# Moving a routing head, two gathers and three turns of gathered rows within the last batches of a retention and expert kernel

## The chip, the core and the metric

The kernel runs on one core of a Trainium2 chip. The metric is the device time of one execution in microseconds (us). Engines are TensorE (PE in the profile; PEld is its weight loads), VectorE (DVE), ScalarE (ACT), GpSimd (POOL) and SyncE (SP), which issues most transfers.

## What is computed

The reference is causal retention followed by a layer of experts with one expert per token:

```python
scores = (q @ k.transpose(0, 1, 3, 2)) / sqrt(64)            # (8, 8, 576, 64) each
ret = scores * Dmat        # Dmat[h, i, j] = gamma[h] ** (i - j) for i >= j, else 0
x = (ret @ v).transpose(0, 2, 1, 3).reshape(4608, 512)
logits = norm(x) @ norm(expert_emb).T / tau                  # 8 experts
expert = argmax(logits, axis=1)
gate = softmax(logits)[token, expert]
out = gate * (relu(x @ w1[expert]) @ w2[expert])             # 512 -> 1024 -> 512
```

All data is float32; the large products are made from high and low parts, each of which TensorE takes at its faster float32 form.

## The kernel before, in words

The work has two stages. The first loops over the eight batches of the retention (b = 0 to 7) and routes tokens to experts on the way; the second loops over the eight experts. Inside a scheduled region the order of each engine's instructions is the order in which the program emits them, so the order is written out by hand, and SP's and POOL's queues keep it too.

For every batch from 1 on the program calls `scores(b)`, `tokens(b - 1)` and `products(b)`. The 576 positions of a batch are four chunks of 128 and a tail of 64; heads go in four pairs.

- `scores(b)`: per pair, `emit_A` (L703) makes the scores within each chunk on TensorE (L709) and evicts them on DVE times the decay (L718); `scale_q` (L697) scales the queries of the pair on POOL (L699), in place, after the scores have read them. At the end `scale_k` (L676) scales the keys of the next batch on POOL, four instructions (L680) that wait for the load of these keys. In batch 7, three gathers (`gather`, L357, POOL's L360) come directly behind the first scaling of queries: each fetches 128 token rows of expert 0 from `xd` in HBM, by the indices `gid`, into the buffers raw2, raw3 and raw6.
- `tokens(b)`: `route_logits` (L892) makes the logits of the batch, evicted by ACT (L903); `route_rank(b - 1)` (L246) ranks the tokens of the batch before within their experts: TensorE multiplies with the one-hots (L256 to L260) into a PSUM bank, DVE adds up the counts (L263, L267), reads the bank (L270), and makes slot numbers (L273 to L284); `route_onehot` (L287) makes two more one-hots on DVE (L292, L300, L307); `route_tile` (L868) turns a tile of 128 tokens on TensorE (L875), copies it on ACT (L876) and stores it to `xd` from SP (L879); `route_turn` (L907) turns the logits and adds them up on DVE (L917). In tokens(6), which stands in front of products(7), `xprep` (L387) follows for each of the three gathered blocks: four transposes on TensorE (L392) into one PSUM bank, a high part by ACT (L384) and a low part by DVE (L385); behind each `w0_load` (L511) issues a load of 512 KB of expert 0's first weights from SP (L513) into the first part of the same raw buffer, which overlaps the gathered rows.
- `products(b)`: `emit_U` (L726) makes the state sums: TensorE (L736) into two PSUM banks, one copy on ACT (L746) and three running sums on DVE (L748). In batch 6 `route_bump`, `route_table(4)` and `slots_to_tokens(0, 3)` (L339 to L350) come next, which make the indices of the three gathers. `emit_O` (L784, L792) makes the outputs within chunks, in two groups of two pairs. `route_squares` (L884) squares the batch's tiles on ACT (L887). In batch 7 `w0_high` (L515) rounds the first two blocks of weights on ACT (L518) and the low parts follow behind `emit_At` on DVE and POOL (L519). `emit_At` (L824) makes the scores of the tail, times the decay on DVE (L833). Then comes the **routing head**, `route_head(b - 1)` (L179): six small DVE instructions (L191, L192, L194, L196, L198, L199) that find each token's expert. `emit_S` (L800, L808) adds the state's part to the outputs, which ACT evicts (L818, L821, L822; DVE the last group of batch 7), and `emit_Ot` (L838, L848) the tail's outputs, evicted by DVE (L859). In batch 7 the head stands behind `emit_Ot`.

PSUM has eight banks. From batch 1 on `Banks.tile` hands them out in one ring, in the order of the calls; whoever writes a bank waits until its former content has been read. After batch 7 the first product of an expert, `mm1_in` (L450, L457), starts; it needs the high and the low parts of the three turned blocks and of the first weights. Between such products stand the logits, ranks, turns and heads of the last batches (L1030 to L1048).

Of the kernel before, what the change touches and what calls it, by code (L numbers as in the profile page):

```python
# [9 lines left out]
F32 = mybir.dt.float32  # L10
# [8 lines left out]
P = 128  # L19
B, H, S, D = 8, 8, 576, 64  # L20
NP = H // 2
NCH = 4
# [71 lines left out]
def retention_moe(ctx: ExitStack, tc: tile.TileContext, qk, kv, w1, w2, head, cst, out):  # L94
# [22 lines left out]
    psa, psm, every = Banks(banks[:4]), Banks(banks[4:]), Banks(banks)  # L117
# [237 lines left out]
    BEG = group_tiles(B - 3)[0] * P  # L355

    def gather(e, i, rows=N):  # L357
        a = e * CT + i
        t = xg[e, i] = raws[(2, 3, 6)[i]] if (e, rows) == (0, BEG) else raws[(i + 1) % 7]
        nc.gpsimd.indirect_dma_start(  # L360
            out=t[:, XO : XO + DM],
            out_offset=None,
            in_=xd[:rows, :],
            in_offset=bass.IndirectOffsetOnAxis(ap=gid[:, a : a + 1], axis=0),
        )
# [18 lines left out]
        nc.scalar.copy(hi, u)  # L384
        nc.vector.tensor_tensor(out=x[:, 1, :, j * P : (j + 1) * P], in0=u, in1=hi.bitcast(F32), op=ALU.subtract)  # L385

    def xprep(e, i):  # L387

        t = xg.pop((e, i))
        ps = psm.tile([P, 512], F32, name="m")  # L390
        for p in range(NP):
            nc.tensor.transpose(ps[:, p * P : (p + 1) * P], t[:, XO + p * P : XO + (p + 1) * P], ident)  # L392
        xsplit(i, ps.rearrange("p (r n) -> p r n", r=NP))
        done(ps)
# [107 lines left out]
    with ExitStack() as att:  # L502
# [8 lines left out]
        def w0_load(c):  # L511
            w0[c] = raws[(2, 3, 6, 5)[c]][:, :1024]
            nc.sync.dma_start(out=w0[c], in_=w1[0, c])  # L513
# [162 lines left out]
        def scale_k(b):  # L676
            g = cc("gneg").rearrange("p (c h) -> p c h", c=NCH)
            k = kview(b).rearrange("p c (h d) -> p c h d", h=H)
            for c in range(NCH):
                nc.gpsimd.tensor_tensor(  # L680
                    out=k[:, c], in0=k[:, c], in1=g[:, c].unsqueeze(2).broadcast_to([P, H, D]), op=ALU.mult
                )
# [42 lines left out]

        def emit_U(b):  # L726
            k, v, T = kview(b), vview(b), Tst
            for c2 in range(NCH // 2):
                ps = psm.tile([P, 512], F32, name="m")
                u = ps.rearrange("p (c r d) -> p c r d", c=2, r=NP)  # L730
                for ci in range(2):
                    c = 2 * c2 + ci
                    for p in range(NP):
                        for h in range(2):
                            hd = 2 * p + h
                            nc.tensor.matmul(  # L736
                                u[h * D : (h + 1) * D, ci, p, :],
                                k[:, c, hd * D : (hd + 1) * D],
                                v[:, c, hd, :],
                                start=True,  # L740
                                stop=True,
                            )
                for ci in range(2):
                    c = 2 * c2 + ci
                    if c == 0:
                        nc.scalar.copy(T[:, 0], u[:, 0])  # L746
                    else:
                        nc.vector.tensor_tensor(out=T[:, c], in0=u[:, ci], in1=T[:, c - 1], op=ALU.add)  # L748

        def emit_U0(g):  # L750
            k, v, T = kview(0), vview(0), Tst
# [212 lines left out]
        def scores(b):  # L964
            for p in range(NP):
                emit_A(b, p)
                scale_q(b, p)
                if (b, p) == (B - 1, 0):
                    for i in range(3):
                        gather(0, i, BEG)  # L970
            if b + 1 < B:
                scale_k(b + 1)

        def tokens(b):
            route_logits(b)
            if b >= 1:
                route_rank(b - 1)
            if 2 <= b < B - 2:
                route_table(b - 2)
            if b >= 1:  # L980
                route_onehot(b - 1)
            for g in range(group_tiles(b)[1]):
                route_tile(b, g)
            route_turn(b)
            if b == B - 2:
                for i in range(3):
                    xprep(0, i)
                    w0_load(i)

        def products(b):  # L990
            end = b == B - 1
            emit_U(b)
            if b == B - 2:
                route_bump()
                route_table(b - 2)
                slots_to_tokens(0, 3)
            emit_O(b, 0)
            emit_O(b, 1)
            route_squares()
            if end:  # L1000
                low = [w0_high(0), w0_high(1, nc.gpsimd)]
                w0_load(3)
            emit_At(b)
            if end:
                for split in low:
                    split()
            else:
                route_head(b - 1)
            emit_S(b, 0)
            emit_S(b, 1)  # L1010
            emit_Ot(b)
            if end:
                split = w0_high(2)
                route_head(b - 1)
                split()
# [13 lines left out]
        b = B - 1  # L1029
# [20 lines left out]
    with ExitStack() as moe:  # L1050
# [98 lines left out]
        highs, lows, held = [], [], []  # L1149
# [179 lines left out]
        b = B - 1  # L1329
# [240 lines left out]
```

## Time and profile before

| what | value |
|---|---|
| median of 3 runs | 571.63 us (570.49 to 573.10) |
| the profiled execution | 571.3 us |
| its span, first to last instruction | 569.3 us |
| busy share of the span, TensorE | 98% |
| weight loads of TensorE | 89% |
| DVE | 74% |
| ACT | 68% |
| POOL | 42% |

The profile is of one execution. Busy time counts the instructions of an engine, overlapping weight loads apart. An arrow `<-` at the end of a row, in brackets, names what ended the idle time in front of it; "issue" is idle time in which the engine waited for nothing that the profile shows. The retention fills the span's first 138 us; the experts follow.

### The profile page before, as it was taken

What the parts mean: (1) busy time and instruction counts of PE and PEld (TensorE: products, weight loads), DVE (VectorE), ACT (ScalarE), POOL (GpSimd) and SP (SyncE); (2) the same over time, 40 slices, a digit from 0 to 9 for tenths busy, and PEclk for the clock granted to TensorE, in tenths of its full rate; (3) what the DMA queues carried; (4) which work ended last, traced back from release to release, by engine and by line L of the source; (5) the groups of instructions that cost most, each with busy time, mean ns of one, the idle gap of its engine ahead of it and who ended that gap; (6) DMA issues with size and microseconds to landing.
All of it is one profiled execution on the core that took longest, in us unless ns stands there. A gap on an engine that the chain in (4) does not pass through costs nothing.

```text
span 569.3 us, 13083 instructions
## 1 busy us (share of the span) xinstructions
PE 558.0 (98%) x5090; PEld 506.5 (89%) x5090; DVE 420.0 (74%) x938; ACT 384.5 (68%) x700; POOL 237.8 (42%) x233
## 2 busy tenths in 40 slices
PE   8999999998999999999999999999999999999995
PEld 8899989887998899889989988998898899889985
DVE  5767767998866878877877878688687878887810
ACT  1345555555749887887787788778878887867511
POOL 6674443574346740552075037306521750342022
PEclk9999999999999999999999999999999999999999
DMA  9999999956567583557457445735655585423211
GB/s 324 413 374 377 364 380 337 384 184 209 181 203 172 183 191 120 168 167 161 130 156 194 129 136 172 172 112 168 181 133 144 168 162 171 116 93 90 70 41 46
DMA packets 72128, 109.22 MB, mean 192 GB/s; under 512 B 42328, under 2 KB 43772, under 8 KB 70272
## 3 DMA queue, kind: packets, MB, share of 16 engines
q1 hardware_dynamic: 62960, 86.24, 48.8%
q0 software_dynamic: 7696, 19.95, 10.8%
q10 hardware_dynamic: 1408, 2.17, 1.1%
q8 instruction: 41, 0.67, 0.5%
q14 instruction: 23, 0.19, 0.1%
HBM read 80.27 MB, written 19.94 MB: 176 GB/s over the span
## 4 chain that ended last, share of the span: by engine, by line
PE 88%; issue 8%; DVE 2%; POOL 1%; DMA 1%; POOLq 0%; ACT 0%; SPq 0%; DVEq 0%
PE m L1248 22%; PE a L1195 15%; PE a L1248 11%; PE m L1195 11%; PE a L457 3%; PE a L709 3%; PE a L792 3%; PE m L792 2%; PE m L709 2%; PE m L457 2%; PE m L875 2%; PE a L736 1%; PE m L736 1%; PE m L808 1%; PE a L875 1%
## 5 line engine op out<-in xcount | busy, mean ns | idle before, releaser
L1248 PE MATMUL m<-w2s,hs 128*128 128x512 f32 x600 | 138.8, 389 | 0.0
L1248 PEld LDWEIGHTS m<-w2s,hs 128*128 128x128 f32 x600 | 112.3, 188 | 22.9
L1261 POOL DMA_INDIRECT out<-y,sid x41 | 47.5, 1159 | 191.9 <-DVE wsum L1117 125.7
L1248 PE MATMUL a<-w2s,hs 128*128 128x512 f32 (+1 forms) x384 | 83.6, 376 | 0.0
L1248 PEld LDWEIGHTS a<-w2s,hs 128*128 128x128 f32 x384 | 68.9, 188 | 13.1
L1195 PE MATMUL a<-xsb,w0s 128*128 128x320 f32 x342 | 58.0, 309 | 0.0
L373 POOL DMA_INDIRECT gt<-gd,gid x40 | 45.1, 1128 | 19.2 <-issue 10.5
L1195 PEld LDWEIGHTS a<-xsb,w0s 128*128 128x128 f32 x342 | 52.1, 188 | 0.0
L360 POOL DMA_INDIRECT raw<-xd,gid x40 | 42.9, 1072 | 20.8 <-DVE sid L350 9.2
L1166 ACT ACTIVATE hs<-y 128x320 fp32r<-128x320 f32 x84 | 39.3, 474 | 17.8 <-DVE y L1207 16.7
L1159 DVE SCALAR_TENSOR_TENSOR hs<-y,hs 128x320 fp32r<-128x320 f32 x84 | 46.7, 569 | 2.0
L408 ACT COPY raw<-raw 128x1024 uint16<-128x1024 uint16 x35 | 47.5, 1356 | 0.0
L443 ACT CAST xsb<-raw 128x128 fp32r<-128x128 f32 x70 | 32.1, 459 | 21.7 <-DVE raw L426 20.9
L680 POOL TENSOR_TENSOR kt<-kt,cs 128x512 f32<-128x512 f32 x28 | 28.3, 1043 | 42.3 <-DMA kt<-kv 42.3
L1094 DVE TENSOR_TENSOR w2s<-raw,w2s 128x1024 fp32r<-128x1024 f32 x32 | 39.1, 1223 | 7.0 <-ACT w2s L1091 7.0
L1207 DVE TENSOR_TENSOR y<-a,y 128x320 f32<-128x320 f32 x47 | 22.8, 488 | 19.9 <-ACT y L1211 13.6
L1091 ACT CAST w2s<-raw 128x1024 fp32r<-128x1024 f32 x32 | 33.4, 1045 | 3.2 <-DMA raw<-w 3.2
L401 ACT COPY raw<-raw 128x1024 uint16<-128x1024 uint16 x35 | 35.4, 1046 | 0.0
L699 POOL TENSOR_TENSOR qkt<-qkt,gsb 128x384 f32<-128x384 f32 x32 | 31.3, 1005 | 7.6 <-PE a L709 4.0
L419 DVE TENSOR_TENSOR raw<-raw 128x256 f32<-128x256 f32 x35 | 14.8, 424 | 26.1 <-ACT raw L408 26.1
L1195 PE MATMUL m<-xsb,w0s 128*128 128x320 f32 x198 | 34.1, 309 | 0.0
L1211 ACT COPY y<-a 128x320 f32<-128x320 f32 x48 | 20.5, 426 | 16.8 <-PE a L1195 12.7
(254 smaller groups left out, 1200.4 us busy)
## 6 DMA issues: line engine op xcount, KB each, us to landing
raw<-w SPq DMA_DIRECT2D x64, 512.0 KB, 3.9
qkt<-qk SPq DMA_DIRECT2D x28, 576.0 KB, 7.3
xd<-y SPq DMA_DIRECT2D x36, 256.0 KB, 9.5
vt<-kv SPq DMA_DIRECT2D x7, 1152.0 KB, 12.9
kt<-kv SPq DMA_DIRECT2D x7, 1024.0 KB, 10.5
qkt<-qk ACTq DMA_DIRECT2D x4, 288.0 KB, 5.4
qkt<-qk SPq DMA_DIRECT2D x4, 288.0 KB, 5.6
out<-y,sid POOLq DMA_INDIRECT x41, 3.1
```

Of the source, the lines that this page charges most:

```text
L360: nc.gpsimd.indirect_dma_start(out=t[:, XO : XO + DM], out_offset=None, in_=xd[:rows, :], in_offset=bass.IndirectOffsetOnAxis(ap=gid[:, a ...
L373: nc.gpsimd.indirect_dma_start(out=g[:, i : i + 1], out_offset=None, in_=gd[:, :], in_offset=bass.IndirectOffsetOnAxis(ap=gid[:, a : a + 1 ...
L401: nc.scalar.copy(far.rearrange("p (h n) -> p h n", h=2), near.rearrange("p (n h) -> p h n", h=2))
L408: nc.scalar.copy(far.bitcast(U16).rearrange("p (n h) -> p h n", h=2), near.rearrange("p (h n) -> p h n", h=2))
L443: nc.scalar.copy(hi, u)
L1091: nc.scalar.copy(hi, u)
L1094: nc.vector.tensor_tensor(out=lo, in0=u, in1=hi.bitcast(F32), op=ALU.subtract)
L1159: nc.vector.scalar_tensor_tensor(out=lo, in0=part(src), scalar=0.0, in1=hi.bitcast(F32), op0=ALU.max, op1=ALU.subtract)
L1166: nc.scalar.activation(hi, part(src), AF.Relu)
L1195: nc.tensor.matmul(ps[:, :HC], w[:, ws, ka, d * P : (d + 1) * P], xop(kx, xsp)[:, d, :], start=(n in (1, 2, 5) and d == 0 and k == 0), sto ...
L1248: nc.tensor.matmul(ps[:, :step], hs[:, hsp, f, i * P : (i + 1) * P], w[:, ws, f, n : n + step], start=(j == 0 and k == 0), stop=(j == NF - ...
L1261: put = nc.gpsimd.indirect_dma_start(out=out.rearrange("t (k n) -> (t k) n", k=k), out_offset=bass.IndirectOffsetOnAxis(ap=rows, axis=0), ...
```

## The change

It takes the two PSUM tiles of the state sums before their first use and hands them back from `emit_U`. The routing head of every batch but the last is called directly behind the state sums instead of behind the scores of the tail; in batch 6 that is in front of `route_bump`, `route_table` and `slots_to_tokens`. In batch 7, gathers 1 and 2 are issued behind the last scaling of queries, gather 0 stays where it was. The turn of gathered block 0, with its weight load, goes behind the state sums, those of blocks 1 and 2 between the two groups of outputs, into the two PSUM banks of the state sums. The head of batch 7's products stays behind `emit_Ot`.

```diff
-    def xprep(e, i):
+    def xprep(e, i, ps=None):
 
         t = xg.pop((e, i))
-        ps = psm.tile([P, 512], F32, name="m")
+        if ps is None:
+            ps = psm.tile([P, 512], F32, name="m")
...
         def emit_U(b):
             k, v, T = kview(b), vview(b), Tst
-            for c2 in range(NCH // 2):
-                ps = psm.tile([P, 512], F32, name="m")
+            held = [psm.tile([P, 512], F32, name="m") for _ in range(NCH // 2)]
+            for c2, ps in enumerate(held):
...
+            return held
...
                 scale_q(b, p)
                 if (b, p) == (B - 1, 0):
-                    for i in range(3):
-                        gather(0, i, BEG)
+                    gather(0, 0, BEG)
             if b + 1 < B:
                 scale_k(b + 1)
+            else:
+                for i in (1, 2):
+                    gather(0, i, BEG)
...
             route_turn(b)
-            if b == B - 2:
-                for i in range(3):
-                    xprep(0, i)
-                    w0_load(i)
+
+        def first_row(i, ps=None):
+            xprep(0, i, ps)
+            w0_load(i)
 
         def products(b):
             end = b == B - 1
-            emit_U(b)
+            held = emit_U(b)
+            if not end:
+                route_head(b - 1)
             if b == B - 2:
                 route_bump()
                 route_table(b - 2)
                 slots_to_tokens(0, 3)
+            if end:
+                first_row(0)
             emit_O(b, 0)
+            if end:
+                for i, ps in enumerate(held, 1):
+                    first_row(i, ps)
             emit_O(b, 1)
             route_squares()
...
             if end:
                 for split in low:
                     split()
-            else:
-                route_head(b - 1)
             emit_S(b, 0)
```

## Rows read from the trace of the kernel before

**Rows 1.** Busy time by stretch: us, busy (instructions) of PE, PEld, DVE, ACT, POOL, clock, DMA, GB/s
```profile
138.50:172.90 34.40, 34.40 (x271) 32.87 (x269) 25.40 (x76) 20.47 (x41) 16.04 (x11) 1.00 0.55 175
```

**Rows 2.** Waits of PE from 20 to 172 us: us in total, times, longest
```profile
PE m L392 <- DVE t L273: 1.3, 1, 1.3
```

**Rows 3.** Timeline of POOL in batch 7: start, us, engine, line, operation, out<-in, count
```profile
121.73 1.18 POOL L360 DMA_INDIRECT raw<-xd,gid  x1 [0.18 <-DVE raw L718]
...
125.46 2.92 POOL L699 TENSOR_TENSOR qkt<-qkt,gsb 128x384 f32<-128x384 f32 x3
```

**Rows 4.** Timeline of DVE in batch 7 and behind it
```profile
125.53 2.89 DVE L267 TENSOR_TENSOR run<-run,s 128x8 bf16<-128x8 bf16 x1
...
129.53 0.83 DVE L292 TENSOR_TENSOR bt<-ai,iota 128x640 bf16<-128x640 int32 x1
...
136.01 1.22 DVE L519 TENSOR_TENSOR w0s<-raw,w0s 128x1024 fp32r<-128x1024 f32 x1
...
142.39 0.24 DVE L331 TENSOR_TENSOR tab<-m,tab 128x80 f32<-128x80 f32 x1 [0.80 <-PE m L258]
...
145.34 0.20 DVE L198 TENSOR_TENSOR oh<-wm,wme 128x40 bf16<-128x40 f32 x1
```

**Rows 5.** Timeline of PE in batch 7 and behind it
```profile
128.87 0.63 PE L392 MATMUL m<-ident,raw 128*128 128x128 f32 x4 [1.32 <-DVE t L273]
...
133.09 1.92 PE L792 MATMUL m<-raw,vt 128*64 128x128 f32 x32
...
138.50 2.36 PE L457 MATMUL a<-xsa,w0s 128*128 128x384 f32 x12
...
145.87 0.19 PE L256 MATMUL m<-oh,stri 128*128 128x40 bf16 x1
```

**Rows 6.** L194 by source line (ns: least/median/most), then DVE's and POOL's timelines beside batch 1
```profile
L194 DVE SCALAR_TENSOR_TENSOR w<-L_all,wme x8: 192/584/969, 35.8 to 144.9; 128x32 f32<-128x32 f32 x4, 128x40 f32<-128x40 f32 x4
...
37.67 1.05 DVE L199 TENSOR_SCALAR tok_all<-wm 128x4 f32<-128x4 f32 x1
...
34.66 4.05 POOL L680 TENSOR_TENSOR kt<-kt,cs 128x512 f32<-128x512 f32 x4 [3.12 <-DMA kt<-kv]
```

**Rows 7.** L360 by source line with landings, then timelines of a later gather and of DVE
```profile
L360 POOL DMA_INDIRECT raw<-xd,gid x40: 944/954/1885, 121.7 to 459.2; - x40
...
DMA to landing us min/median/max: 3.3/3.7/5.6
...
157.62 1.89 POOL L360 DMA_INDIRECT raw<-xd,gid  x1 [0.19 <-issue]
...
157.39 1.22 DVE L1094 TENSOR_TENSOR w2s<-raw,w2s 128x1024 fp32r<-128x1024 f32 x1
```

**Rows 8.** ACT's squares (first, last) and rounding, SP's loads; landings of weight loads
```profile
130.90 0.64 ACT L887 ACTIVATE junk<-y 128x512 bf16<-128x512 f32 x1
...
133.70 0.19 ACT L887 ACTIVATION_READ_ACCUMULATOR junk<-y 128x1 f32 x1
134.40 1.05 ACT L518 CAST w0s<-raw 128x1024 fp32r<-128x1024 f32 x1 [0.51 <-DMA raw<-w]
...
128.03 7.35 SPq L513 DMA_DIRECT2D raw<-w  x4
...
raw<-w SPq DMA_DIRECT2D x64, 512.0 KB, 3.9
```

**Rows 9.** Timeline of PEld in the tokens of batch 1, one of two such rows
```profile
43.36 0.42 PEld L875 LDWEIGHTS m<-ident,xT 128*128 128x128 f32 x4 [0.18 <-DVE raw L718]
```

**Rows 10.** Timelines of POOL, DVE and PEld in batch 6's products
```profile
113.50 4.04 POOL L680 TENSOR_TENSOR kt<-kt,cs 128x512 f32<-128x512 f32 x4 [5.97 <-DMA kt<-kv]
...
112.62 0.88 DVE L748 TENSOR_TENSOR Tst<-m,Tst 128x256 f32<-128x256 f32 x2
...
117.67 0.41 DVE L833 TENSOR_TENSOR pt<-a,cd 128x256 f32<-128x256 f32 x1
...
118.53 0.26 PEld L848 LDWEIGHTS m<-pt,vt 64*64 64x64 f32 x8
```

## The prediction

> **What bounds the kernel now.** I first read the busy time by stretch. From 138.5 us on TensorE is busy for all 34.40 us of the stretch [rows 1]: behind batch 7 it has no hole, so the end can only move by what TensorE gains or loses before that point. Second, the waits of TensorE between 20 and 172 us: one wait for another engine stands there, 1.3 us in the turning of gathered rows (L392) for DVE's L273 [rows 2]; its other holes are "issue", where the profile shows nothing waited for, and the change removes nothing of those. Third, the queues of POOL and DVE around that wait. POOL issues three gathers and only then does the last three scalings of queries, 125.46 to 128.38 [rows 3]. The count of the one-hots on DVE (L267), which reads two SBUF operands, starts at 125.53 and takes 2.89 us [rows 4]: it ends with the third scaling. Behind it in DVE's queue stands the read that gives the ranking's bank back, and the third turn wanted that bank. So TensorE paid 1.32 us, at 128.87 [rows 5], for the order on POOL. The same thing on a smaller scale: L194 of the routing head (two SBUF operands) takes 0.19 us alone and up to 0.97 us [rows 6], beside a scaling of keys; L199, one operand, took 1.05 us in the same place in batch 1's head [rows 6].
>
> **The change, part by part.**
>
> *The PSUM tiles of the state sums taken up front, and two of them used again for turned rows.* The ring is walked in the same order; two fewer banks are taken. No instruction is added: nothing. The cover is that DVE has read both banks before TensorE returns to them; worked out below, it has.
>
> *Gathers 1 and 2 behind the scalings.* On POOL gather 0 ends at 122.91 (121.73 + 1.18); three scalings take 2.92 us [rows 3], so they end at 125.83 where they ended at 128.38. L267 then waits for the last of them alone: it ends at about 125.88 instead of 128.42, 2.54 us earlier, and everything behind it on DVE with it. The 1.32 us on TensorE are gone. Gather 1 follows at about 126.0, gather 2 (0.95 us and a gap of 0.2 on [rows 7]) at 127.2; a gather lands 3.7 us after its start in the median, 5.6 at most [rows 7]: 130.9 for the second.
>
> *The turns moved between sums and outputs.* Same work, other place. From the start of the second pair of outputs to the first expert product TensorE takes 138.50 - 133.09 = 5.41 us [rows 5]. Without the 1.32 us the product could start at 137.18, the second pair of outputs at 131.77, and a turn costs 0.55 us, so TensorE wants gather 2 at 131.22, after its landing at 130.9. What is late next? The gather could be. DVE's L292, also with two SBUF operands, now runs from 126.99 to 127.82 (129.53 less 2.54, 0.83 us [rows 4]), and gather 2 starts inside it. A gather that started 0.23 us into the two-operand L1094 took 1.89 us instead of the median 0.95 [rows 7]: it waited until that instruction ended. Here 0.6 us would be left: landing 131.5, and TensorE waits w = 0.2. I take that, as the row is of the same kind; the ends are 0 and, with a landing of 5.6 us, 1.6.
>
> The Trainium skill (SBUF — State Buffer, "Who interferes with whom") infers that a tensor_tensor of DVE holds only the shared read interface while a gather's descriptors need the write interface, so that it shouldn't delay one. By that w would be 0 and the sum 0.2 us lower; the 1.89 us speak against it.
>
> *The weight loads behind the turns.* The squares (2.99 us, 130.90 to 133.89) and the rounding of the first weights on ACT, 1.05 us [rows 8], now stand behind the third turn's copy, taken as 0.6 us: 131.77 + 0.6 + 2.99 + 1.05 = 136.4, and DVE's low part (1.22 [rows 4]) ends at 137.6 + w, 0.4 us later than before (137.23). The first expert product needs it in its third matmul, due at 137.18 + 0.4: just met. So 1.3 us of slack are used up. Load 0 is issued at about 128.9 (the first turn's end) instead of 128.03; before, it landed about 6.3 us on, when ACT's wait ended at 134.40 [rows 8], now then at 135.2, before ACT is free at 135.35. Load 1 is issued at 131.2: at 3.9 us (the median of 64 such loads [rows 8]) it is hidden; at 6.3 it comes at 137.5, 1.1 us after ACT wants it, and ACT's copies of the first outputs wait behind it, which the batch's logits need: some 0.5 us more. I take 0, since no stores stand in front of it on SP any more; 0.5 belongs to the range.
>
> Then DVE sets the pace. From the end of its first low part to the end of L198 at 145.54 are 8.31 us, of which at least 0.80 waiting for TensorE [rows 4]: 7.5 us of work, so L198 ends at 145.1 + w. The ranking that needs it started on TensorE at 145.87 [rows 5] and could now start at 144.55. So 0.55 us of the 1.32 are given back here. Batch 7: 1.32 - 0.55 - 0.2 = about **-0.6 us** (from -1.3, nothing given back, to +1.3, with the late gather and the late load).
>
> *The routing head behind the state sums.* In batch 1 the head stood beside scaling and held the evictions of batch 2's scores back; TensorE's turns of tiles waited for them, 0.18 us at 43.36 and as long once more behind it [rows 9]. That goes: -0.4. In the other batches TensorE waits for no eviction behind the head: nothing. In batch 6 it can lose. The sums end there at 113.50 (112.62 + 0.88), and in the same moment POOL starts four scalings of keys, 113.50 to 117.54 [rows 10]. Now, four waiting instructions of the slots' arithmetic absorb these, and the decay product (L833) starts at 117.67, ends at 118.08, and TensorE's tail outputs want it at 118.53 [rows 10]. After the change the head's L192, L194, L198 and L199 meet the four scalings, one each, and the head ends at 117.57; behind it come the slots' nine small instructions, unheld (0.17 each, 1.5 us) and the product, 0.41: 119.4, so TensorE is 0.9 us late. But it comes 0.4 earlier from batch 2: if the scalings, which wait for a load, do not move, L192 slips in ahead of them, one scaling is left for a later instruction, and the end is only about 0.3 late against before. Bounds for the end of batch 6: -0.4 (no meeting) to +0.9. I take **+0.3**, the case that moves with TensorE and not with the load.
>
> **Sum.** +0.3 - 0.6 = -0.3 us. The profiled execution took 571.3 us, span 569.3 and 2.0 around it: 571.0. The three runs shown have a median of 571.63, from 570.49 to 573.10, so this execution lies 0.3 under the median. That the two stretches differ by less than the runs scatter is the forecast: no measurable change. About 0.5%, 2.9 us, is what a measurement of this kernel can tell from no change.
>
> **Rivals.**
>
> *All of it arrives* (0.22). Neither the low parts nor the head are ever late: -0.4 - 1.3 = -1.7, 569.6. For it: the weights' loads may land in 3.9 us and the scalings of keys in batch 6 may start later. Against it: DVE's chain behind the first low part.
>
> *The head is caught by the scalings of keys* (0.18), the other side. Place: DVE behind batch 6's sums. The price: if L192 loses every boundary between scalings, as L267 did for 2.89 us, it waits to 117.57, the rest of the head takes 1.0, the slots 1.5, the product 0.4: 120.5 against 118.53, +2.0; with the gain of batch 7, 572.7; without, 573.3. It decides as soon as scalings start before L192 (0.25 us behind the sums). For it: L267. Against it: in batches 1 to 5 each held instruction of the head ended with one scaling [rows 6].
>
> The Trainium skill (SBUF — State Buffer, "SBUF: two separate sides") calls the port between DVE and GpSimd an exclusive lock, held for one whole instruction by whoever starts first. By that L267 would have waited about 1.0 us and not 2.89, and this rival would cost 0.9 instead of 2.0; the trace shows both lengths.
>
> *The gather or the second load is late* (0.10). Landing at 5.6 us gives w = 1.6; the load adds 0.5: 571.3 + 0.3 - 0.6 + 1.9 = 572.9.
>
> The forecast, both effects half undone, keeps 0.50; its own range is 570.2 to 572.2.
>
> **How the numbers follow.** The range goes from the first rival less run scatter to the second plus little: 569.3 to 573.3. Over 2.9 us either way needs more than any single mechanism gives, or a shift of the holes called issue: faster 0.08, same 0.86, slower 0.06.
>
> **What would show it.** Right: L267 of batch 7 at 0.2 to 0.5 us; no wait of L392 for DVE; ACT's rounding of the first weights ending about 136.4 and TensorE's first expert product slowed or started near 137.2; DVE without idle time from there to L198; L192, L194, L198 in batch 6 near 1 us each and L833 later than 118. Wrong: if the first expert product starts 1.5 us earlier and its ranking too (all arrives), if L392 waits for a gather, or if TensorE idles over 1 us in front of batch 6's tail outputs. And all of it is wrong if the stretch behind 138.5 changes its own length.

## The result and the profile after

| | median | runs | ratio to the kernel before, 95% interval |
|---|---|---|---|
| before | 570.52 us (568.91 to 573.48) | 22 | |
| after | 574.47 us (570.62 to 579.12) | 22 | 1.0053 [1.0037, 1.0069] |

The change costs about 3 us by the ratio, 0.53% (4 us between the two medians). The forecast was 571.0 with a range up to 573.3; it was wrong. The profiled execution of the changed kernel took 579.12 us (span 577.1), the longest of its 22, so it shows the loss large; the same kernel profiled a second time ("again" below) took 573.98. One run of head_back (692.5 us) and one of the kernel before (815.9 us), both at a much lower granted clock, stand in none of the ratios.

Waits of TensorE over the whole span, changed kernel: line waited for, us in total, times, longest. [Rows 2] held the wait for DVE's L273 instead.

```profile
PE m L393 <- DMA raw<-xd,gid: 2.4, 1, 2.4
```

The wait for DVE is gone, as meant, and a wait for a gather of 2.4 us stands in its place. The timeline of TensorE in batch 7 of the changed kernel has it (against [rows 5]; L393, L794, L458 are L392, L792, L457 of before):

```profile
131.00 1.39 PE L737 MATMUL m<-vt,kt 128*64 128x64 f32 x40
132.62 0.32 PE L737 MATMUL m<-vt,kt 128*64 128x64 f32 x3 [0.24 <-issue]
133.34 0.85 PE L737 MATMUL m<-vt,kt 128*64 128x64 f32 x21 [0.40 <-issue]
134.12 0.66 PE L393 MATMUL m<-ident,raw 128*128 128x128 f32 x4
134.71 1.97 PE L794 MATMUL a<-raw,vt 128*64 128x128 f32 x32
136.60 0.66 PE L393 MATMUL m<-ident,raw 128*128 128x128 f32 x4
139.63 1.09 PE L393 MATMUL m<-ident,raw 128*128 128x128 f32 x4 [2.37 <-DMA raw<-xd,gid]
140.65 3.09 PE L794 MATMUL a<-raw,vt 128*64 128x128 f32 x32
...
148.43 1.06 PE L902 MATMUL a<-xT,E 128*32 128x512 f32 x8
```

The third turn waits for gather 2 from 137.26 to 139.63. Then it takes 1.09 us where the second took 0.66, and the second pair of outputs 3.09 us where the first took 1.97, for the same 32 matmuls. The busy time by stretch says why; its eighth number is the granted clock:

```profile
137.00:140.60 3.60, 1.23 (x7) 0.74 (x5) 0.69 (x1) 0.58 (x1) 0.00 (x0) 0.86 0.66 239
140.60:143.60 3.00, 3.00 (x33) 2.85 (x32) 0.69 (x1) 2.75 (x8) 0.00 (x0) 0.60 0.52 176
143.60:149.00 5.40, 5.40 (x120) 4.59 (x120) 4.12 (x11) 4.55 (x9) 2.81 (x2) 1.00 0.30 104
```

Behind the idle time TensorE ran for a while at the lower of its two levels, 1.2 instead of 2.4 GHz (mean 0.60 in the second row; 1.00 from 134.10 to 137.00), and was back at full clock behind it. Where gathers 1 and 2 stand is seen on POOL's timeline of the changed kernel (against [rows 3]):

```profile
130.59 1.00 POOL L360 DMA_INDIRECT raw<-xd,gid  x1 [0.17 <-issue]
131.89 1.36 POOL L360 DMA_INDIRECT raw<-xd,gid  x1 [0.31 <-issue]
```

and what they meet on SP's and on DVE's timelines (two fences; the second answers to [rows 4]):

```profile
129.97 1.81 SPq L881 DMA_DIRECT2D xd<-y  x4
```

```profile
130.05 0.40 DVE L267 TENSOR_TENSOR run<-run,s 128x8 bf16<-128x8 bf16 x1
...
131.60 0.83 DVE L292 TENSOR_TENSOR bt<-ai,iota 128x640 bf16<-128x640 int32 x1
```

L267 takes 0.40 us instead of 2.89. But between 129.97 and 131.78 SP issues four stores of 256 KB to `xd`, the tiles of `tokens(6)`, gather 1 is issued among them and gather 2 right behind. The transfers of the changed kernel from 131.7 to 133.0, by queue (q1 carries SP's transfers, q0 the gathers; packets, MB, share of the 16 engines' time):

```profile
q1 hardware_dynamic: 249, 0.45, 94.4%
q0 software_dynamic: 1, 0.00, 5.6%
```

While gather 1 has been issued, 249 packets of stores go and one of the gather's, which starts at 132.9. Not all of that is the stores' doing: with the stores out of the way (stores_behind, below) the first packet of this gather comes 0.6 us into the answering stretch, so the stores put it off by some 0.6 us. Behind it both queues go side by side; the changed kernel from 134.25 to 134.75:

```profile
q0 software_dynamic: 33, 0.12, 58.4%
q1 hardware_dynamic: 36, 0.07, 37.8%
```

**Where the time went.** One length sorts all kernels below: from the start of batch 7's scores to the start of the logits behind the first expert product (L710 and L902 in the changed kernel). It was 21.57 us before and is 24.67 here. What lies behind it is the same: 428.5 us before, 428.7 after. So [rows 1]'s reading holds, and the loss is batch 7's, +3.1 us. (What lies in front is 119.2 and 123.8 us. Of these 4.5 us, 2.3 are idle time in more and longer stops called "issue", one of them 1.64 us at L810, and 2.2 are longer busy time; the other profiles have 118.3 to 120.8 in front.) A second profile with batch 7 as before, that of head_alone below, has a stretch of 20.14, so the 3.1 may be too small by up to 1.4. The parts of the 3.1: the wait for the gather 2.37; the lower clock 1.12 and 0.43, by the rows above; two stops called "issue" inside the state sums, 0.64; gone are the old wait of 1.32 and a stop of 0.73, also "issue", that the kernel before had in the tail of batch 7. That makes 2.5; most of the other 0.6 us is found below.

### The profile page after: what moved, and what is told of

Read it like the earlier page. It is cut to its first block, busy times and chain, and to the rows that moved or that the text cites. A ratio compares the mean times of both kernels' runs of the same rounds, so it can differ in the third digit from the quotient of the medians.

```text
span 577.1 us, 13084 instructions
## 1 busy us (share of the span) xinstructions
PE 562.5 (97%) x5090; PEld 510.0 (88%) x5090; DVE 414.4 (72%) x938; ACT 384.1 (67%) x700; POOL 234.7 (41%) x233
## 4 chain that ended last, share of the span: by engine, by line
PE 85%; issue 8%; DMA 2%; POOL 2%; DVE 2%; ACT 1%; POOLq 0%; SPq 0%; DVEq 0%; ACTq 0%
PE m L1257 17%; PE a L1257 16%; PE m L1204 14%; PE a L1204 13%; PE a L710 4%; PE a L458 2%; PE m L710 2%; PE a L794 2%; PE m L794 2%; PE m L458 2%; DMA raw<-xd,gid 1%; PE m L877 1%; PE a L877 1%; PE a L737 1%; PE m L737 1%
## 5 line engine op out<-in xcount | busy, mean ns | idle before, releaser
L1257 PE MATMUL m<-w2s,hs 128*128 128x512 f32 (+1 forms) x528 | 119.3, 384 | 0.0
L1257 PEld LDWEIGHTS m<-w2s,hs 128*128 128x128 f32 x528 | 97.4, 188 | 19.4
L1257 PE MATMUL a<-w2s,hs 128*128 128x512 f32 (+1 forms) x456 | 103.1, 384 | 0.0
L1257 PEld LDWEIGHTS a<-w2s,hs 128*128 128x128 f32 x456 | 83.9, 188 | 16.7
L360 POOL DMA_INDIRECT raw<-xd,gid x40 | 43.4, 1086 | 19.8 <-issue 7.9
L373 POOL DMA_INDIRECT gt<-gd,gid x40 | 42.5, 1062 | 18.5 <-issue 10.5
L1204 PE MATMUL a<-xsb,w0s 128*128 128x320 f32 x294 | 49.3, 309 | 0.0
L1204 PEld LDWEIGHTS a<-xsb,w0s 128*128 128x128 f32 x294 | 44.7, 188 | 0.0
L1204 PE MATMUL m<-xsb,w0s 128*128 128x320 f32 x246 | 41.6, 309 | 0.0
L1204 PEld LDWEIGHTS m<-xsb,w0s 128*128 128x128 f32 x246 | 37.5, 188 | 0.0
L1204 PE MATMUL m<-xsb,wsa 128*128 128x320 f32 x198 | 33.8, 309 | 0.0
```

Source lines behind the costliest of these rows:

```text
L360: nc.gpsimd.indirect_dma_start(out=t[:, XO : XO + DM], out_offset=None, in_=xd[:rows, :], in_offset=bass.IndirectOffsetOnAxis(ap=gid[:, a ...
L373: nc.gpsimd.indirect_dma_start(out=g[:, i : i + 1], out_offset=None, in_=gd[:, :], in_offset=bass.IndirectOffsetOnAxis(ap=gid[:, a : a + 1 ...
L1204: nc.tensor.matmul(ps[:, :HC], w[:, ws, ka, d * P : (d + 1) * P], xop(kx, xsp)[:, d, :], start=(n in (1, 2, 5) and d == 0 and k == 0), sto ...
L1257: nc.tensor.matmul(ps[:, :step], hs[:, hsp, f, i * P : (i + 1) * P], w[:, ws, f, n : n + step], start=(j == 0 and k == 0), stop=(j == NF - ...
```

## The experiments

Each group of kernels had its own runs of the kernel before, whose medians were 571.4 (head_back, head_alone, gathers_early and again), 572.0 (loads_behind to gather2_later) and 572.0 (the last four). "Stretch" is the length just defined, "rest" what lies behind it, both in the one profiled execution; a 0.001 of the ratio is 0.57 us.

| kernel | median, us | ratio [95% interval] | stretch, us | rest, us |
|---|---|---|---|---|
| before | 570.5 | 1 | 21.57 | 428.5 |
| after | 574.47 | 1.0053 [1.0037, 1.0069] | 24.67 | 428.7 |
| again (after once more) | 573.53 | 1.0038 [1.0017, 1.0059] | 23.79 | 428.9 |
| head_back | 574.71 | 1.0056 [1.0028, 1.0084] | 21.73 | 429.0 |
| head_alone | 570.89 | 0.9992 [0.9977, 1.0007] | 20.14 | 428.6 |
| gathers_early | 572.93 | 1.0028 [1.0008, 1.0047] | 21.97 | 428.9 |
| loads_behind | 574.12 | 1.0044 [1.0017, 1.0071] | 23.61 | 428.9 |
| squares_first | 571.60 | 0.9994 [0.9973, 1.0015] | 20.75 | 428.5 |
| gathers_first | 570.03 | 0.9958 [0.9933, 0.9982] | 18.73 | 428.6 |
| gather2_later | 575.42 | 1.0059 [1.0035, 1.0084] | 24.57 | 428.4 |
| stores_behind | 574.27 | 1.0029 [0.9998, 1.0060] | 21.14 | 430.5 |
| front_all | 571.49 | 0.9987 [0.9964, 1.0010] | 20.59 | 428.8 |
| front_squares | 571.05 | 0.9976 [0.9950, 1.0001] | 19.35 | 429.5 |
| front_head | 569.54 | 0.9953 [0.9925, 0.9981] | 18.99 | 428.7 |

### again: the change once more

> The changed kernel once more, for a second profile. In the first one TensorE waited 2.4 us for the second of the two late gathers, the granted clock fell behind that wait, and batch 6's tail came 0.6 us later against before. Theory A (late gather): the wait for the gather is there again, 1.5 to 3 us, and time over before is 2 to 4 us. Theory B (the routing head is caught by the scalings of keys in batch 6): the wait in batch 7 is small or absent this time, and batch 6 loses 1 us or more.

0.4% slower again, and its wait of L393 for the gather was 1.93 us. TensorE kept its full clock behind that one (1.00 in every stretch), and the second pair of outputs took its 1.97 us. Without the clock's loss another wait is to be seen; TensorE's timeline of this second execution:

```profile
134.79 0.63 PE L393 MATMUL m<-ident,raw 128*128 128x128 f32 x4 [1.93 <-DMA raw<-xd,gid]
...
139.92 0.62 PE L458 MATMUL m<-xsa,w0s 128*128 128x384 f32 x2 [0.22 <-ACT w0s L519]
141.18 2.00 PE L458 MATMUL m<-xsa,w0s 128*128 128x384 f32 x10 [0.64 <-DVE w0s L520]
```

The first expert product waits 0.86 us for the rounded weights. In the slower execution above, these came in time because TensorE was later still.

Something other than stores stands in front of the gather's end here. Two rows of this execution's transfers from 132.25 to 134.2 (q8, "instruction", carries fetches of instructions, 16 KB each):

```profile
q0 software_dynamic: 4, 0.01, 3.3%
q8 instruction: 1, 0.02, 2.8%
```

The fetch starts at 132.26; no packet of a gather starts between 132.3 and 133.1, and the last four follow it, behind 133.1. In the first execution the last one likewise follows a fetch, after a gap from 137.4 to 138.25. So some 0.9 us of the gather's lateness there, and up to 1.9 here, stand behind a fetch and not behind stores (that fetch and packets share a DMA engine is read from their times alone). In loads_behind, below, no fetch stands near the gather's end.

### head_back and head_alone: which half loses?

head_back is the changed kernel with the head at its old place; head_alone is the kernel before with the head moved.

```diff
# head_back, against after          # head_alone, against before
-            if not end:              +            if not end:
-                route_head(b - 1)    +                route_head(b - 1)
...
+            else:                    -            else:
+                route_head(b - 1)    -                route_head(b - 1)
```

> The changes of batch 7 alone: the routing head stands behind the scores of the tail again, in all batches. Theory A: all of the loss stays, +2 to +4 us over the kernel before, with TensorE waiting 1.5 to 3 us for a gather. Theory B: the loss goes, within 0.5 us of before, or a gain up to 1 us.

> The kernel before with nothing but the routing head moved directly behind the state sums; gathers and turns as before. Theory A: within 1 us of the kernel before (-0.4 from batch 2, up to +0.9 in batch 6). Theory B: +2 us or more.

The whole loss stays with the first and none with the second: it is batch 7's part. The head does meet the scalings of keys in batch 6; DVE's timeline of head_alone there:

```profile
114.14 0.74 DVE L198 TENSOR_TENSOR oh<-wm,wme 128x40 bf16<-128x40 f32 x1
114.80 1.05 DVE L199 TENSOR_SCALAR tok_all<-wm 128x5 f32<-128x5 f32 x1
...
116.88 0.96 DVE L342 SCALAR_TENSOR_TENSOR t<-t,tab 128x3 f32<-128x3 f32 x1
```

L191 to L196 slip in ahead of the scalings, four instructions behind them (these and L339, 0.57 us) wait for one scaling each, and TensorE waits 0.3 us for the product of L833 (0.6 to 1.2 in nine other profiles with the moved head, nothing in that of after). In head_alone this costs no measurable time as a whole. head_back's profiled execution happened to be its fastest, 571.13 us; it shows no wait for a gather at all, while other runs of it go up to 579.4. So this wait differs from run to run, and it does so with the stores in the same place: in the stretch of this profile that answers to the one shown above, 250 packets of stores go and one of the gather's.

### gathers_early and gather2_later: is it the gathers' lateness?

```diff
# gathers_early, against after
-                    gather(0, 0, BEG)
+                    for i in range(3):
+                        gather(0, i, BEG)
...
-            else:
-                for i in (1, 2):
-                    gather(0, i, BEG)
# gather2_later, against after; gsb isn't read any more
-                for i in (1, 2):
-                    gather(0, i, BEG)
+                gather(0, 1, BEG)
+                for _ in range(2):
+                    nc.gpsimd.tensor_tensor(out=gsb[:, 0, :], in0=gsb[:, 0, :], in1=gsb[:, 1, :], op=ALU.mult)
+                gather(0, 2, BEG)
```

> The changed kernel with all three gathers directly behind the first scaling of queries, as before; the turns stay between sums and outputs. DVE's L267 is held again by the three scalings, 2 to 3 us, but TensorE has the state sums to do in the meantime. Theory A: the gathers land 3.5 us after their start, before any load of weights is issued, no turn waits for one, and the time is 0 to 1.5 us under the kernel before. Theory B: the loss stays, +2 us or more.

> The changed kernel with two idle multiplications (2 us) on POOL between gathers 1 and 2; the products of these are read by nothing. The state sums of batch 7 took 3.2 us instead of 2.1 in all three profiles with late gathers, with two stops called issue, while gather 2 stood on POOL. If the gather's issue stops TensorE's instructions, the stops go from the state sums (2.1 us again) and stand elsewhere or nowhere. If they belong to this place in the program, the sums take 3.2 us again. The time itself will be 1 to 3 us above the changed kernel, as the third turn waits longer.

With gather 2 issued 2.0 us later (3.28 us behind gather 1 instead of 1.30), the wait for it is 2.88 us and the clock falls again; its ratio can't be told from the change's own, 1.0053, and its stretch (24.57) is 0.8 to 1.0 longer than those of again and loads_behind but no longer than that of after, so the two multiplications didn't show as a clean extra in the end. The stops in the state sums, which the run was made to place, are absent (2.08 us for the sums), but they are absent in loads_behind too, where gather 2 wasn't moved; that a gather's issue causes them is not shown. With the gathers back in front of the scalings no gather is waited for, yet the kernel is still 0.28% slower than before, 1.6 us, between what the two theories had. TensorE's timeline of gathers_early:

```profile
131.40 0.66 PE L393 MATMUL m<-ident,raw 128*128 128x128 f32 x4 [0.67 <-DVE Tst L749]
132.39 0.66 PE L393 MATMUL m<-ident,raw 128*128 128x128 f32 x4 [0.33 <-DVE Tst L749]
```

L267 is held by the scalings again (2.30 us), the running sums behind it are late, and now the turns wait 1.0 us for them, since they take the banks of the state sums. The weights' 0.86 us come on top, as in again. So this run doesn't price the gathers alone: it brings the old hold back in another form.

### loads_behind: do the weight loads hold the gather?

```diff
-            w0_load(i)
+            if i == 2:
+                for c in range(3):
+                    w0_load(c)
```

> The changed kernel with the three loads of first weights behind the third turn instead of one behind each turn. What makes gather 2 late? Theory A1 (the load issued in front of it takes its place on the DMA engines): no turn waits for a gather, at most 0.3 us, and the last gather packet ends about 12.5 us behind the start of batch 7's scores, as it did at 12.9 in the run with the head back; the first expert product then waits longer for its weights, 2 us or more instead of 0.9. Theory A2 (the burst of stores and the fetch of instructions, which ran on one DMA engine just in front of the gather's last packets in both slow profiles): the wait is there in some runs all the same, 1 to 2.5 us.

The edit moved nothing. In the schedule a load waits only for the turn that frees its buffer, and SP issued the first one 9.95 us behind the start of batch 7's scores, as in other kernels of the series. So this is in effect a third copy of the change: wait 2.43 us, clock at 0.53 behind it, outputs in 3.16 us. It tells nothing of the loads; stores_behind does that below. One thing it adds: the state sums had no stop called "issue" here, so those 0.64 us come and go and are not the change's.

### squares_first: the weights' wait

gathers_early, with the squares called behind the first turn:

```diff
             if end:
                 first_row(0)
+                route_squares()
             emit_O(b, 0)
```

> The kernel with early gathers, with ACT's squares moved in front of the first outputs, where ACT stood idle for 2.6 us, so that the rounding of the first weights comes 2.6 us earlier. It costed +1.6 us over the kernel before. If the wait of the first expert product for its weights (0.86 us on TensorE in three of the profiles) is what the turns between the outputs cost, it goes, and the time falls by 0.7 to 1.2 us, to within 1 us of the kernel before. If not, the time stays within 0.3 us of the kernel with early gathers.

The wait of the first expert product is gone, and the kernel is level with the one before: 572.93 to 571.60 by the medians (ratio 1.0028 to 0.9994), 21.97 to 20.75 in the stretch. The 0.86 us of idle time are worth 1.2, as the stops also break up a run of matmuls: the product's 12 take 2.35 us in one run here and 0.62 and 2.02 in two in gathers_early.

### gathers_first: the first idea alone, done on POOL

The kernel before, with all three gathers in front of the first scaling. Nothing is turned elsewhere.

```diff
                 emit_A(b, p)
-                scale_q(b, p)
                 if (b, p) == (B - 1, 0):
                     for i in range(3):
                         gather(0, i, BEG)
+                scale_q(b, p)
```

> The kernel before with the three gathers in front of the first scaling of queries in batch 7, where POOL stood idle for 3.0 us; nothing else. If the 1.3 us of TensorE were owed to the scalings of queries standing behind the gathers, L267 waits 0.6 us or less instead of 2.9, the third turn waits for nothing, and the time is 0.8 to 1.5 us under the kernel before. If the wait only goes to something else (a gather's landing, an eviction), the time is within 0.5 us of before.

0.42% faster than before. POOL's timeline of this kernel, then TensorE's:

```profile
117.71 1.18 POOL L360 DMA_INDIRECT raw<-xd,gid  x1 [0.18 <-DVE t L349]
...
121.42 3.89 POOL L699 TENSOR_TENSOR qkt<-qkt,gsb 128x384 f32<-128x384 f32 x4
```

```profile
126.12 1.48 PE L392 MATMUL m<-ident,raw 128*128 128x128 f32 x12
127.53 2.09 PE L736 MATMUL a<-vt,kt 128*64 128x64 f32 x64
129.44 1.92 PE L792 MATMUL a<-raw,vt 128*64 128x128 f32 x32
131.19 1.92 PE L792 MATMUL m<-raw,vt 128*64 128x128 f32 x32
133.04 0.62 PE L831 MATMUL m<-qkt 64*64 64x64 f32 x14
```

Before, POOL stood idle for 3.0 us ahead of its first scaling of batch 7; its timeline of the kernel before:

```profile
120.55 1.00 POOL L699 TENSOR_TENSOR qkt<-qkt,gsb 128x384 f32<-128x384 f32 x1 [3.01 <-issue]
```

The gathers fit there: their packets have gone when those of the stores begin, the scalings end at 125.31 and L267 starts at 125.28 and takes 0.17 us. All twelve transposes run in one piece. This is the 1.32 us of [rows 2] without anything late in exchange. The stretch is 2.8 us shorter than that of before, whose "issue" stop of 0.73 is absent too, and 1.4 shorter than head_alone's.

### stores_behind, front_all, front_squares, front_head: what holds the gathers, and what the rest costs

```diff
# stores_behind, against after: route_tile keeps the store of tokens(6) back
+            if b != B - 2:
+                store(xw, t)
...
                 first_row(0)
+                for xw, t in squares:
+                    store(xw, t)
# front_all, against after: the order of gathers_first on POOL
-                scale_q(b, p)
                 if (b, p) == (B - 1, 0):
-                    gather(0, 0, BEG)
+                    for i in range(3):
+                        gather(0, i, BEG)
+                scale_q(b, p)
...
-            else:
-                for i in (1, 2):
-                    gather(0, i, BEG)
# front_squares: front_all with the edit of squares_first
# front_head: gathers_first with the edit of head_alone
```

> The changed kernel, with the four 256 KB stores of batch 6's token rows emitted behind the first turn and its weight load instead of in front of the state sums; on SP's queue the load waits for that turn, so the stores should be issued some 4 us later (about 11 to 13 us behind the start of batch 7's scores, instead of 6.2 to 8.0). Theory A (the late gathers land late because the stores' data is moved in front of theirs): the packets of gathers 1 and 2 end by 11.5, TensorE's wait for them falls from 1.9-2.9 us to under 0.8, the clock stays at 2.4 GHz, and the time is that of the kernel with early gathers or better: 1.5 to 4 us less than the changed kernel, a ratio of 0.998 to 1.003. Rival B (they land late because POOL issues them late and every gather of this place takes 5 us): the wait stays near 2 us, the time near 1.005. Rival C (the weight loads or instruction fetches hold them): the packets still end behind 13.5, the wait stays over 1.5 us.

> The changed kernel with all three gathers in front of the first scaling of queries; the turns between state product and outputs and the head stay as the change has them. Theory A (the changed kernel loses by the landing, 2 to 3.5 us with the clock, then 0.86 us for the wait of the first expert product for its weights and 1.0 us of turns behind a late DVE): no wait for gathers, the adding-up of ranks (L267) not held, so the turns wait for nothing either; 0.86 us of weights' wait stays, and 0.3 to 0.9 us of batch 6's head: against the kernel before -1.32 + 0.86 + 0 to 0.5, a ratio of 0.998 to 1.001. Rival B (the turns between state product and outputs cost by themselves, with batch 7's order or the banks handed on): slower than the kernel before by 1.5 us or more, 1.002 to 1.005.

> As front_all, with the squares of batch 6's tiles on ACT called behind the first turn instead of behind the outputs, so that the first expert product's weights are rounded earlier. Theory A: the weights' wait of 0.86 us goes too: 0.996 to 0.999, about 0.9 us below front_all. Rival B (the squares then delay the copies of the turned blocks on ACT by as much, or the product waits for DVE anyway): no difference from front_all, within 0.4 us.

> The kernel before with the gathers in front of the first scaling (0.9958 by itself) and with the routing heads behind the state sums, as the change has them (0.9992 by itself). If the two are independent: 0.9950, -2.9 us. If the head meets DVE's work of batch 6 in front of the gathers' indices, which now are wanted 3 us earlier on POOL: the first gather starts up to 0.5 us later and the gain of the gathers falls by as much, 0.996 to 0.997.

**stores_behind** keeps the late gathers, to 0.01 us at the same places behind the start of batch 7's scores (6.84 and 8.14 us), and takes the stores out of their way. Its transfers in the 1.3 us that answer to those shown above for the changed kernel (127.46 to 128.76; the first row is the busy share of the DMA engines in 40 slices, in tenths):

```profile
DMA  0000000000000000009699099800000300336999
...
q0 software_dynamic: 29, 0.12, 44.4%
```

The packets are gather 1's, the first at 128.05. The time of a gather from its issue to its landing is the last number of the next rows: gather 1 and gather 2 here, then gather 1 in loads_behind, where the stores stand in front.

```profile
raw<-xd,gid POOLq DMA_INDIRECT x1, 3.3
raw<-xd,gid POOLq DMA_INDIRECT x1, 4.5
raw<-xd,gid POOLq DMA_INDIRECT x1, 4.8
```

Gather 1 took 5.1 in gather2_later. For gather 2, TensorE went on 7.7, 7.3 and 6.7 us after its issue in after, again and loads_behind. TensorE's timeline of this kernel, and ACT's:

```profile
132.32 0.63 PE L393 MATMUL m<-ident,raw 128*128 128x128 f32 x4 [0.41 <-DMA raw<-xd,gid]
```

```profile
138.99 1.05 ACT L519 CAST w0s<-raw 128x1024 fp32r<-128x1024 f32 x1 [1.59 <-DMA raw<-w]
```

The wait falls from 1.9 to 2.9 us to 0.41, and the clock stays at 1.00 (the outputs behind take 1.97 us): the stores are a part of what the gathers landed behind. How large a part of the wait it is, one profile doesn't settle, as head_back had no wait with the stores in front. The ratio is 1.0029 [0.9998, 1.0060], at the upper end of what was expected and not distinct from no gain: the stores now stand in front of the second block of weights, ACT waits 1.59 us for it, DVE's work is late in its turn, and the next rankings wait twice 0.5 us for L198; the rest is 430.5 us where the others have 428.4 to 429.5. One collision was exchanged for another, so this run shows the mechanism and not its price.

**front_all** gives the price: with early gathers the otherwise unaltered change is at 0.9987 [0.9964, 1.0010], against 1.0038 to 1.0053 for its three copies. The two kernels differ by the gathers' place alone. So the late gathers cost some 0.5 to 0.7%, 2.9 to 3.8 us, give or take 0.3%. The weights' wait stays (0.91 us here), and **front_squares** takes 1.24 us from the stretch, though only 0.4 us of it show in the medians, within their scatter; a wait of 0.43 us for L198 comes up behind it.

What is left between front_squares (19.35) and gathers_first (18.73) is the turns' new place. TensorE's timeline of front_all, to be read beside that of gathers_first:

```profile
126.98 2.08 PE L737 MATMUL m<-vt,kt 128*64 128x64 f32 x64
129.00 0.66 PE L393 MATMUL m<-ident,raw 128*128 128x128 f32 x4
129.59 1.97 PE L794 MATMUL a<-raw,vt 128*64 128x128 f32 x32
131.49 1.09 PE L393 MATMUL m<-ident,raw 128*128 128x128 f32 x8
132.51 1.97 PE L794 MATMUL a<-raw,vt 128*64 128x128 f32 x32
```

There turns, state sums and outputs take 6.92 us (126.12 to 133.04) in three blocks; here 7.43 (126.98 to 134.41, where L833 starts) in five, with no wait between them (7.42 in front_squares, 6.92 in front_head): 0.5 us for the same work in more pieces.

**front_head** leaves the turns where they were, and has early gathers and the moved head: 0.9953 [0.9925, 0.9981], 569.54 us against 572.03, the lowest ratio of the series and faster than both kernels. The two parts look independent (0.9958 and 0.9992 by themselves), though the head's share can't be told from nothing.

## Why the prediction was wrong

**Right.** L267 fell from 2.89 to 0.40 us (0.2 to 0.5 was named), and TensorE's 1.32 us for L273 went. The head meets the scalings in batch 6 much as in the case taken: L192 slips in ahead of them (L194 too), each of four later instructions waits for one, and TensorE's tail outputs are 0.3 us late in head_alone (0.6 to 1.2 in nine other profiles). Nothing measurable came out of it in head_alone's time, and the second rival (head caught, +2.0) fell with head_alone. The stretch behind kept its length.

**Wrong: the term w.** The step that failed is "a gather lands 3.7 us after its start in the median, 5.6 at most", and from it w = 0.2 us. Gather 2 was taken as landing at 131.5; what happened was a wait of 1.93 to 2.88 us in four of the five profiled copies or near copies of the change. The third rival had the mechanism, at a chance of 0.10 and with w = 1.6 at most. The 3.7 us came from 40 gathers of the whole kernel [rows 7], most of them in the stage of the experts. It was too short for this gather even without stores: the last of the three landed 4.3 to 5.7 us after its issue in squares_first, front_squares, front_all, front_head and gathers_first, all with early gathers. The four stores were in the kernel before, at the end of `tokens(6)`, and I moved two gathers past them on the DMA engines while I looked at POOL's and DVE's queues alone. front_all, which differs from the change by the gathers' place alone, shows that this place is what the change loses by, about 3 us. Why a gather lands late there is shown in part: the stores hold it (gather 1 by 1.5 to 1.8 us, by the three landings above, one profile each), and in after and again its last packets also followed a fetch of instructions. What each adds to the wait stays open.

The Trainium skill (DMA: Bandwidth & Descriptors, "Queues, rings and completion order") says that each DMA engine takes turns between its queues packet by packet. By that the gather's packets go in alternation with the stores' once both are there, and the 33 and 36 packets in half a microsecond above agree with it, if the profile counts the same packets. The 249 to 1 ahead of them says little against it: in the first 0.6 of its 1.3 us the gather's first packet wasn't due. Why the stores went alone from 132.3, when it was, to 132.9, no run here shows.

**Missing: the clock.** No term stood for what idle time does to TensorE's clock. Behind waits of 2.37, 2.43 and 2.88 us it ran at 1.2 GHz for a while, behind 1.93 and 0.41 it didn't; where it fell, the same 32 matmuls took 3.04 to 3.16 us and not 1.97.

**Mis-sized: the weights.** "Just met" was worked out with 5.41 us on TensorE from the second pair of outputs to the first expert product. That stretch of the kernel before holds a stop; its timeline of TensorE there:

```profile
137.67 0.33 PE L808 MATMUL m<-qkt,Tst 64*64 64x128 f32 x2 [0.73 <-issue]
```

I counted it as TensorE's work. In front_squares, which stops there for nothing, the same stretch takes 4.3 us (133.54 to 137.83), and 4.2 in head_alone and gathers_first, which have the order of before. So the product could start a good deal earlier than the 137.18 of the prediction, the weights' low part couldn't, and in front_all the product waits 0.91 us.

**Mis-sized: the turns.** "Same work, other place" was costed at nothing; in five pieces it takes 0.5 us more.

By these, for the change: -1.3 for the old wait, +0.5 for the pieces, +1.9 to +2.9 for the gather, and either +0.9 for the weights (again) or up to 1.6 for the clock: 2.0 to 3.7. The measured +3.0 lies among these. An execution without a wait, such as head_back's profiled one, loses next to nothing.

## What to carry to other kernels

Before a transfer is moved to a later place, list what every other queue issues in front of that place, and take the landing time from an instance with the same traffic ahead of it, not from the median of all; a wait that some executions have and others don't needs more than one profile. To take away a hold between two engines, first look for a hole on the engine that holds: here POOL idled for 3 us just ahead, and the gathers in that hole gave 0.42% with three lines moved. Slack that is read off a stretch with a stop called "issue" isn't slack, since the stop may not come back.

## What the runs showed of the hardware

- The lower clock behind single waits of 2.37 to 2.88 us, in a kernel whose TensorE is busy for 97% of the span. In the profile after it took 1.5 us beside the wait's 2.4.
- Stores of one queue put off a gather of another that is issued among them: its first packet by some 0.6 us, its landing from 3.3 to 4.8 and 5.1 us after its issue (gather 1 in stores_behind, loads_behind, gather2_later).
- A fetch of instructions (q8, 16 KB, 0.9 and 1.2 us) can stand in front of the last packets of a gather: they came up to 1.9 us (again) and 0.9 us (after) behind the others.
- On POOL gather 2 took 1.36 us where most take 0.95, beside DVE's L292 with two SBUF operands (131.60 to 132.43). It ended 0.82 us behind the end of that instruction, as the gather of [rows 7] ended 0.90 behind L1094's, so the hold that the prediction took from there is there, 0.41 us and not the 0.6 that it had. The inference of the Trainium skill (SBUF — State Buffer, "Who interferes with whom") that a tensor_tensor doesn't hold a gather's descriptors isn't borne out by this row either.
- A stop costs TensorE more than its idle time: with the weights' wait of 0.86 and 0.91 us gone, the stretch was 1.2 us shorter (gathers_early to squares_first, front_all to front_squares).
